# Squared-ReLU attention and an ELU MLP on one core: transposed score tiles turned a step earlier, loaded into up to four tiles, and no longer used in the last block

## The chip, the cores and the metric

The kernel runs on 1 core of one Trainium2 chip. The metric is device time in microseconds. The kernel before takes 2069.99 us, the median of 3 runs (2069.19 to 2071.52).

## The reference

```python
# u, v: (4, 3008, 256); z: (4, 3008, 64); moe_w_in: (256, 2048); moe_w_out: (2048, 256)
scores = (1.0 / S) * np.matmul(z, z.transpose(0, 2, 1))
attn = np.maximum(scores, 0.0) ** 2
x = (u * np.matmul(attn, v)).reshape(B * S, D)
h = x @ w_in
g = np.where(h > 0.0, h, np.exp(np.minimum(h, 0.0)) - 1.0)
out = g @ w_out
```

All arrays are float32. The score matrix of a batch is symmetric, since both of its factors are z.

## The kernel before

Every float32 operand of a matmul is split into a high part and the rest (`hi`, `lo`), and a product is the sum of three: high by high, high by low, low by high. The program has two stages. The attention stage takes the first 1096 us of the profiled execution, the MLP stage the rest; the change lies in the first.

The attention stage walks over 4 batches. A batch has 6 blocks of 496 or 512 columns of the score matrix (`BLOCKS`), and a block has 12 steps. A step handles one pair of 128-row strips, 256 rows, against the block's columns. So there are 288 steps, numbered by `s`; block 0 to block 5 of a batch follow each other, and `ORDER` says which pair stands at which place of a block. A step has three parts:

- `a_front(s)`: six matmuls of 64 rows, two beside each other, make the scores of the pair in PSUM tile `banks[s % 2]` (called `f`).
- `a_mid(s)`: ScalarE takes the ReLU out of `f` into half a row of SBUF (`r_two[s % 2]`), squares it there, ScalarE (pairs in `BY_ACT`) or VectorE makes `hi` from it, and VectorE subtracts to get `lo`. `hi` and `lo` each lie in a ring of three buffers.
- `a_back(s)`: 24 matmuls, twelve of them after each other with two running beside each other, add the pair's products with v to the four accumulators `acc`. `products` sets their order: the triple (c, d, q) names strip, half of the output and product (q = 1 is the one that reads `lo`). The last step of a block has nine in place of twelve.

Since the scores are symmetric, some of them exist already when a later block of the batch asks for them. Blocks 1 to 5 take the pairs in `LOADED` not from matmuls but from HBM, where `p_store` put them in an earlier block: 2, 4, 6, 6 and 4 pairs, 22 a batch, 88 in all. Such a loaded step has no `a_front`. `p_load(s)` fetches it with four DMAs of 128 KB, rows of 64 elements, into `r_two[s % 2]`; it is put two steps ahead of its use. In `a_mid(s)` VectorE then turns it by 32 x 32 squares (STREAM_TRANSPOSE, L478) into PSUM tile `banks[s % 2]`, ScalarE copies `hi` out of it, and VectorE subtracts.

Every engine runs its instructions in the order in which the program was written. The loop over `t` at L877 writes, for each step: `a_front(t)`, `a_back(t - 2)`, `a_mid(t)`, and then `background(t)`, the jobs that the table `at` gave to that step: loads and splits of v and z, the split of the MLP's weights (`w_split`, one or two VectorE instructions a step in blocks 1 to 3 of the first batches), and the splits and stores of what the attention stage yields (`x_parts`, `x_split`). All attention loads and most stores are issued by SyncE's queue, in order. At the second step of a block, `a_sums` adds the last block's accumulators (ScalarE copies two, VectorE adds two), before which the new block's first products can't start.

The last block of the last batch runs into the MLP stage: `START` lists the first MLP instructions and the products of steps 285 to 287 between them, and GpSimd's queue loads the MLP's inputs (`x_load`) into v's tiles as they come free.

## Time and profile before

| | |
|---|---|
| time, median of 3 runs | 2069.99 us |
| profiled execution: time, span | 2070.43 us, 2068.7 us |
| busy over the span: TensorE, VectorE, ScalarE | 94%, 83%, 72% |
| granted TensorE clock, mean | 0.981 |
| chain that ended last, by engine | TensorE 61%, ScalarE 14%, VectorE 10%, DMA 7%, issue 5% |
| DMA packets; of these under 512 B | 280431; 194528 |

The profile's page gives shares over the whole span, so it averages the two stages. Busy time of TensorE's matmuls contains time in which a matmul that has been started waits inside the pipeline, so it can't be read as work done. To see a stage, the busy time of each engine is asked for by windows; to see why an engine stands, the timeline of that window names, in brackets, the idle time ahead of an instruction and what ended it.

### The profile page before, as it was taken

To read this page: it belongs to the slowest core of one execution; us is meant where nothing else is said; L and a number is where in the kernel's file an instruction comes from. 1 tells how busy PE (TensorE), PEld (TensorE's weight loads), DVE (VectorE), ACT (ScalarE), POOL (GpSimd) and SP (SyncE) were. 2 spreads that over 40 slices of the span, in tenths; PEclk is the share of its full clock that TensorE was granted. 3 is DMA by queue.
4 is the path that set the end of the run, shared out by engine and by line. 5 is a ranking of instruction groups with operands and counts; after the bars stand their busy time and mean duration, and the time that the engine had idled before them with its cause. 6 is when DMAs were issued, how large, how long until landed. Compare 5 with 4: busy or idle time off the path is not lost.

```text
span 2068.7 us, 30697 instructions
## 1 busy us (share of the span) xinstructions
PE 1935.0 (94%) x12302; PEld 1584.9 (77%) x12302; DVE 1712.1 (83%) x1692; ACT 1493.0 (72%) x1629; POOL 60.8 (3%) x88
## 2 busy tenths in 40 slices
PE   9988889888899888998869999999999999999999
PEld 6876677766687666876657888888888888888887
DVE  7776677766678666876658999999999999999998
ACT  8765577656686556876548778788778787777887
POOL 0000000000000000000000000000000100000100
PEclk9999999999999999999989999999999999999999
DMA  7464756646566555556581123222221211211210
GB/s 237 164 172 119 186 176 217 185 118 166 147 232 196 147 128 155 213 183 150 119 218 50 45 75 105 61 74 78 76 71 50 71 60 30 91 60 30 73 38 20
DMA packets 280431, 247.60 MB, mean 120 GB/s; under 512 B 194528, under 2 KB 243936, under 8 KB 280288
## 3 DMA queue, kind: packets, MB, share of 16 engines
q1 hardware_dynamic: 260880, 202.39, 32.9%
q0 software_dynamic: 19264, 43.13, 7.6%
q8 instruction: 96, 1.57, 0.3%
q14 instruction: 47, 0.39, 0.1%
q10 hardware_dynamic: 144, 0.13, 0.0%
HBM read 138.17 MB, written 107.41 MB: 119 GB/s over the span
## 4 chain that ended last, share of the span: by engine, by line
PE 61%; ACT 14%; DVE 10%; DMA 7%; issue 5%; SPq 2%; DVEq 0%; ACTq 0%
PE p L674 12%; PE acc L392 11%; PE acc L693 8%; PE acc L691 8%; PE acc L692 8%; PE r L674 6%; ACT row L184 5%; DMA row<-p 5%; DVE row L181 4%; ACT row L487 4%; ACT row L484 4%; DVE f L478 4%; PE q L674 3%; PE f L392 3%; SPq L430 2%
## 5 line engine op out<-in xcount | busy, mean ns | idle before, releaser
L392 PE MATMUL acc<-row,x 64*128 64x496 f32 (+1 forms) x6768 | 845.8, 396 | 53.8 <-DVE row L181 31.9
L392 PEld LDWEIGHTS acc<-row,x 64*128 64x128 f32 x6768 | 659.5, 190 | 213.3 <-DVE row L181 56.9
L181 DVE TENSOR_TENSOR row<-row,row 128x992 fp32r<-128x992 f32 (+7 forms) x366 | 498.5, 1367 | 142.1 <-ACT row L184 134.0
L184 ACT ACTIVATE row<-p 128x496 f32<-128x496 f32 (+1 forms) x384 | 225.3, 587 | 130.1 <-PE p L674 120.4
L184 ACT ACTIVATE row<-f 128x992 fp32r<-128x992 f32 (+1 forms) x88 | 88.1, 1001 | 308.6 <-DVE f L478 288.7
L691 PE MATMUL acc<-row,wo_hi 128*128 128x496 f32 (+1 forms) x768 | 295.4, 385 | 0.0
L692 PE MATMUL acc<-row,wo_hi 128*128 128x496 f32 (+1 forms) x768 | 295.4, 385 | 0.0
L693 PE MATMUL acc<-row,wo_lo 128*128 128x496 f32 (+1 forms) x768 | 295.4, 385 | 0.0
L766 DVE SCALAR_TENSOR_TENSOR row<-row,row 128x1984 f32<-128x1984 f32 (+5 forms) x104 | 217.0, 2086 | 24.2 <-ACT row L764 23.8
L484 ACT ACTIVATE row<-f 128x992 f32<-128x992 f32 (+1 forms) x199 | 199.7, 1003 | 40.6 <-PE f L392 23.0
L760 ACT ACTIVATE row<-row 128x1984 f32<-128x1984 f32 (+5 forms) x104 | 182.2, 1752 | 58.4 <-DVE row L758 56.3
L768 DVE SCALAR_TENSOR_TENSOR row<-row,row 128x1984 f32<-128x1984 f32 (+5 forms) x103 | 216.0, 2097 | 0.2
L487 ACT ACTIVATE row<-row 128x992 f32<-128x992 f32 (+1 forms) x199 | 208.1, 1046 | 5.6
L181 DVE TENSOR_TENSOR row<-f,row 128x992 fp32r<-128x992 f32 (+1 forms) x88 | 105.1, 1195 | 100.3 <-ACT row L184 100.3
L762 ACT ACTIVATE row<-row 128x1984 f32<-128x1984 f32 (+5 forms) x104 | 181.6, 1747 | 0.5 <-DVE row L768 0.2
L764 ACT ACTIVATE row<-row 128x1984 f32<-128x1984 f32 (+5 forms) x104 | 181.4, 1746 | 0.3
L674 PE MATMUL p<-x,wi_hi 128*128 128x496 f32 (+1 forms) x576 | 175.0, 385 | 0.0
L693 PEld LDWEIGHTS acc<-row,wo_lo 128*128 128x128 f32 x768 | 144.2, 188 | 26.5
L692 PEld LDWEIGHTS acc<-row,wo_hi 128*128 128x128 f32 x768 | 144.2, 188 | 26.4
L691 PEld LDWEIGHTS acc<-row,wo_hi 128*128 128x128 f32 x768 | 144.2, 188 | 26.4
L184 ACT ACTIVATE row<-row 128x992 fp32r<-128x992 f32 (+3 forms) x157 | 143.7, 925 | 8.8 <-DVE row L768 2.9
L478 DVE STREAM_TRANSPOSE f<-row 128x1024 f32<-128x1024 f32 x88 | 110.5, 1256 | 42.8 <-DMA row<-p 40.2
(89 smaller groups left out, 1981.9 us busy)
## 6 DMA issues: line engine op xcount, KB each, us to landing
row<-p SPq DMA_DIRECT2D x352, 128.0 KB, 3.0
p<-row SPq DMA_DIRECT2D x72, 512.0 KB, 2.9
x<-x POOLq DMA_DIRECT2D x56, 496.0 KB, 4.6
x<-row SPq DMA_DIRECT2D x69, 248.0 KB, 2.7
x<-x POOLq DMA_DIRECT2D x28, 512.0 KB, 5.0
p<-row SPq DMA_DIRECT2D x24, 496.0 KB, 3.1
row<-in_v SPq DMA_DIRECT2D x44, 256.0 KB, 3.5
x<-row SPq DMA_DIRECT2D x38, 256.0 KB, 2.6
```

The lines of the kernel that those rows point to most:

```text
L181: nc.vector.tensor_tensor(out=lo, in0=src, in1=hi.bitcast(F32), op=ALU.subtract)
L184: nc.scalar.activation(out=out, in_=in_, func=AF.Copy)
L392: nc.tensor.matmul(out, w[rows], x[rows], start=start, stop=end)
L478: nc.vector.transpose(out=x.rearrange("p c (g j) -> p c g j", g=16), in_=t)
L484: nc.scalar.activation(out=x, in_=f[:, :, :n], func=AF.Relu, scale=1.0 / S)
L487: nc.scalar.activation(out=x, in_=x, func=AF.Square)
L674: nc.tensor.matmul(o, w, x, start=first and i == 0, stop=i == 2, skip_group_check=not first)
L691: nc.tensor.matmul(o, wh, hi, start=first, stop=False)
L692: nc.tensor.matmul(o, wh, lo, start=False, stop=False)
L693: nc.tensor.matmul(o, wl, hi, start=False, stop=last)
L766: stt(out=t, in0=m, scalar=1.0, in1=t, op0=ALU.add, op1=ALU.mult)
L768: stt(out=h, in0=h, scalar=0.0, in1=t, op0=ALU.max, op1=ALU.add)
```

## The change

`LOADED` loses its entries for block 5, whose `ORDER` becomes the natural one: all twelve of its steps make their scores by matmul. Block 1 of the last batch does so too. Loaded steps go from 88 to 70.

A planner, run while the program is written, now gives each step its tile (`t_of`) out of up to four: the two halves of `row3` as before, and in blocks 1 to 4 also the row `lr` and half of `row8` (the last batch has no `row8`). It also says when a load is issued (`at_of`): as early as four steps ahead, where a tile is free. In the plan that results every load is issued three or four steps ahead. `early(s)` holds for all 70.

The turning moves into `p_turn`. For an early step `s + 1` it is written into `a_mid(s)`, ahead of step s's subtraction, so it stands one step earlier in VectorE's order. The last two loaded steps of a block (30 in all) are turned into an SBUF tile (`x_of`) in place of a PSUM bank.

`products` puts those that read `lo` last. In the start of the program, four products of step 0 go ahead of step 1's scores. Loads and splits of z and v for the next batch move a little, since block 5's order is another.

```diff
-CLOSING = (0, 1, 2, 3, 6, 7, 4, 8, 9, 5, 10, 11)
+CLOSING = NATURAL
-LOADED = ((), (10, 11), (8, 9, 10, 11), (6, 7, 8, 9, 10, 11), (6, 7, 8, 9, 10, 11), (6, 7, 8, 9))
+LOADED = ((), (10, 11), (8, 9, 10, 11), (6, 7, 8, 9, 10, 11), (6, 7, 8, 9, 10, 11), ())
+AHEAD = 4
...
-    def products(late, edge):
-        if late:
-            return [(c, d, q) for q in (0, 2, 1) for c in range(2) for d in range(KD)]
-        if edge:
-            return [(c, d, q) for d in range(KD) for c in range(2) for q in range(3)]
-        return [(c, d, q) for c in range(2) for d in range(KD) for q in range(3)]
+    def products(i, first):
+        if i == NP - 1:
+            return [(c, d, q) for d in range(KD) for c, q in ((0, 0), (0, 2), (0, 1), (1, 0), (1, 1), (1, 2))]
+        if i == 0 and not first:
+            return [(c, d, q) for d in range(KD) for q in (0, 2, 1) for c in range(2)]
+        return [(c, d, q) for q in (0, 2, 1) for c in range(2) for d in range(KD)]
...
     def is_loaded(s):
-        return pair_of(s) in LOADED[s // NP % NI]
+        k = s // NP
+        return pair_of(s) in LOADED[k % NI] and k != (B - 1) * NI + 1
...
+    def p_turn(s):
+        order = "p (g c j) -> p c g j" if pair_of(s) == NP - 1 else "p (g j c) -> p c g j"
+        t = t_of[s].rearrange(order, g=16, c=2)
+        nc.vector.transpose(out=turned(s).rearrange("p c (g j) -> p c g j", g=16), in_=t)
+
+    def turned(s):
+        return pairs(x_of[s]) if s in x_of else banks[s % 2]
+
+    t_of, at_of, x_of = {}, {}, {}
+    tiles = r_two + [lr_row, cut(st_row, 0, 2)]
...
+    def early(s):
+        return s < NSTEP and is_loaded(s) and at_of[s] <= s - 3
...
-            x = banks[s % 2]
-            order = "p (g c j) -> p c g j" if pair_of(s) == NP - 1 else "p (g j c) -> p c g j"
-            t = r_two[s % 2].rearrange(order, g=16, c=2)
-            nc.vector.transpose(out=x.rearrange("p c (g j) -> p c g j", g=16), in_=t)
-            x = x[:, :, :n]
+            if not early(s):
+                p_turn(s)
+            if early(s + 1):
+                p_turn(s + 1)
+            x = turned(s)[:, :, :n]
             copy(hi[:, :, :n], x)
...
+            if early(s + 1):
+                p_turn(s + 1)
             nc.scalar.activation(out=x, in_=x, func=AF.Square)
...
-            at(s - 2, p_load, s)
+            at(at_of[s], p_load, s)
```

VectorE in the last four steps of block 3 of the first batch, before. `f0` and `f1` are the two PSUM banks, `row3` holds the two halves that loads fill, `row0` to `row2` hold `hi` and `lo`; the rows with `wi_` and `wt` are the split of the MLP's weights.

```order
L478 STREAM_TRANSPOSE f0_100<-row3_73 128x1024
L181 TENSOR_TENSOR row0_70<-f0_100,row0_70 128x2x496
L320 SCALAR_TENSOR_TENSOR wi_hi_63<-wm0_82,wt_84 128x512
L478 STREAM_TRANSPOSE f1_101<-row3_73 128x1024
L181 TENSOR_TENSOR row1_71<-f1_101,row1_71 128x2x496
L322 TENSOR_SCALAR wt_84<-wi_hi_63 128x512
L324 SCALAR_TENSOR_TENSOR wi_lo_64<-wt_84 128x512
L478 STREAM_TRANSPOSE f0_100<-row3_73 128x1024
L181 TENSOR_TENSOR row2_72<-f0_100,row2_72 128x2x496
```

Each turn is followed by the subtraction that reads the same bank. The same place now:

```order
L437 STREAM_TRANSPOSE f1_101<-row8_79 128x1024
L182 TENSOR_TENSOR row0_70<-f0_100,row0_70 128x2x496
L321 SCALAR_TENSOR_TENSOR wi_hi_63<-wm0_82,wt_84 128x512
L437 STREAM_TRANSPOSE lr_80<-row3_73 128x1024
L182 TENSOR_TENSOR row1_71<-f1_101,row1_71 128x2x496
L323 TENSOR_SCALAR wt_84<-wi_hi_63 128x512
L325 SCALAR_TENSOR_TENSOR wi_lo_64<-wt_84 128x512
L437 STREAM_TRANSPOSE row8_79<-row3_73 128x1024
L182 TENSOR_TENSOR row2_72<-lr_80,row2_72 128x2x496
```

The turn ahead of a subtraction is now that of the next step, and the last two write SBUF (`lr`, `row8`).

VectorE in the last block of the last batch, before, from the first step whose place is taken by a loaded pair:

```order
L478 STREAM_TRANSPOSE f0_100<-row3_73 128x1024
L181 TENSOR_TENSOR row2_72<-f0_100,row2_72 128x2x496
L181 TENSOR_TENSOR row4_74<-row4_74,high_81 128x496
L478 STREAM_TRANSPOSE f1_101<-row3_73 128x1024
L181 TENSOR_TENSOR row0_70<-f1_101,row0_70 128x2x496
L181 TENSOR_TENSOR row4_74<-row4_74,lr_80 128x496
L492 CAST row1_71<-row3_73 128x2x496
```

And now:

```order
L535 CAST row2_72<-row3_73 128x2x496
L182 TENSOR_TENSOR row2_72<-row3_73,row2_72 128x2x496
L182 TENSOR_TENSOR row4_74<-row4_74,row8_79 128x496
L182 TENSOR_TENSOR row0_70<-row3_73,row0_70 128x2x496
L182 TENSOR_TENSOR row4_74<-row4_74,high_81 128x496
L535 CAST row1_71<-row3_73 128x2x496
```

No turn is left there; `hi` of some steps is a cast by VectorE, of others a copy by ScalarE.

SyncE's queue around the same four steps of block 3, before (`p` are the stored scores, x4 is one loaded step):

```order
L577 DMA x0_1177<-high_81 128x512
L578 DMA x0_1177<-row4_74 128x512
L252 DMA row7_78<-in_zz 128x496
L287 DMA wm1_83<-in_w_in 128x1024
L430 DMA row3_73<-p01_107 32x16x64 x7
L430 DMA row3_73<-p00_106 32x16x64 x9
```

And now:

```order
L432 DMA row3_73<-p01_107 32x16x64 x4
L620 DMA x0_1174<-high_81 128x512
L621 DMA x0_1174<-row4_74 128x512
L432 DMA row8_79<-p01_107 32x16x64 x3
L432 DMA row8_79<-p00_106 32x16x64
L253 DMA row7_78<-in_zz 128x496
L288 DMA wm1_83<-in_w_in 128x1024
L432 DMA row3_73<-p00_106 32x16x64 x8
```

Two of the four loads have moved past the load of weights and the store of a split part, and one of them goes to `row8`.

## Rows read from the trace of the kernel before

**Rows 1.** Windows: blocks 0 to 5 of batch 1; blocks 1 on; the last block.

```profile
core 0: us, PE busy (x) PEld busy (x) DVE busy (x) ACT busy (x) POOL busy (x), PEclk, DMA share, GB/s
280.10:321.20 41.10, 40.72 (x356) 32.80 (x356) 34.16 (x50) 35.99 (x48) 0.00 (x0) 1.00 0.61 222
321.20:365.90 44.70, 41.93 (x354) 33.94 (x352) 34.17 (x46) 30.75 (x35) 0.00 (x0) 0.96 0.63 205
365.90:410.60 44.70, 39.88 (x344) 31.64 (x340) 34.25 (x43) 28.03 (x33) 0.00 (x0) 1.00 0.66 192
410.60:458.00 47.40, 39.36 (x312) 30.03 (x314) 32.49 (x40) 26.10 (x31) 0.00 (x0) 0.96 0.54 139
458.00:503.70 45.70, 40.26 (x324) 31.47 (x323) 30.68 (x34) 27.60 (x34) 0.00 (x0) 0.96 0.54 137
503.70:554.40 50.70, 41.08 (x314) 31.87 (x312) 32.98 (x42) 32.99 (x46) 0.00 (x0) 0.90 0.58 152
48.40:280.10 231.70, 200.06 (x1643) 160.99 (x1641) 162.35 (x198) 143.98 (x168) 0.00 (x0) 0.97 0.56 157
595.90:825.30 229.40, 201.31 (x1654) 157.90 (x1652) 163.79 (x201) 145.24 (x171) 0.00 (x0) 0.97 0.58 163
865.40:1042.60 177.20, 159.96 (x1332) 126.38 (x1328) 121.38 (x136) 114.96 (x132) 0.00 (x0) 0.97 0.55 156
1042.60:1096.30 53.70, 37.76 (x278) 28.93 (x276) 29.20 (x33) 27.76 (x34) 4.27 (x7) 0.84 0.67 174
```

**Rows 2.** Timeline of TensorE: steps made by matmul, 512 columns (start, us, engine, line).

```profile
18.78 3.10 PE L392 MATMUL acc<-row,x 64*128 64x512 f32 x24
21.50 1.06 PE L392 MATMUL f<-q,row 64*128 64x512 f32 x6
...
307.14 2.88 PE L392 MATMUL acc<-row,x 64*128 64x512 f32 x24
309.86 0.84 PE L392 MATMUL f<-q,row 64*128 64x512 f32 x6
310.54 1.75 PE L392 MATMUL acc<-row,x 64*128 64x512 f32 x14
```

**Rows 3.** Timeline of all engines: loaded steps of block 3, first batch.

```profile
171.65 3.35 PE L392 MATMUL acc<-row,x 64*128 64x496 f32 x24 [0.73 <-DVE row L181]
172.11 1.25 DVE L478 STREAM_TRANSPOSE f<-row 128x1024 f32<-128x1024 f32 x1
173.46 1.00 ACT L184 ACTIVATE row<-f 128x992 fp32r<-128x992 f32 x1 [3.09 <-DVE f L478]
174.49 1.19 DVE L181 TENSOR_TENSOR row<-f,row 128x992 fp32r<-128x992 f32 x1 [1.13 <-ACT row L184]
...
175.60 0.42 DVE L322 TENSOR_SCALAR wt<-wi_hi 128x512 int32<-128x512 int32 x1
...
175.74 2.73 PE L392 MATMUL acc<-row,x 64*128 64x496 f32 x22 [0.73 <-DVE row L181]
...
176.05 0.69 DVE L324 SCALAR_TENSOR_TENSOR wi_lo<-wt 128x512 fp32r<-128x512 int32 x1
176.66 1.25 DVE L478 STREAM_TRANSPOSE f<-row 128x1024 f32<-128x1024 f32 x1
```

**Rows 4.** Groups of instructions, attention stage: ScalarE's square and ReLU (busy, mean ns | idle).

```profile
L487 ACT ACTIVATE row<-row 128x992 f32<-128x992 f32 x112 | 115.7, 1033 | 3.1
L484 ACT ACTIVATE row<-f 128x992 f32<-128x992 f32 x112 | 110.8, 989 | 8.3 <-PE f L392 5.7 <-DMA p<-row 1.5 <-DVE row L551 0.5
```

**Rows 5.** Waits over the span (us in total, times, longest).

```profile
ACT row L184 <- DVE f L478: 288.7, 83, 8.5
DVE f L478 <- DMA row<-p: 40.2, 29, 5.9
```

**Rows 6.** DMA issues: size each, median us from issue to landing.

```profile
row<-p SPq DMA_DIRECT2D x352, 128.0 KB, 3.0
```

**Rows 7.** Timeline of the last block: a load issued, and a turn.

```profile
1053.41 2.23 SPq L430 DMA_DIRECT2D row<-p  x4
...
1061.14 1.26 DVE L478 STREAM_TRANSPOSE f<-row 128x1024 f32<-128x1024 f32 x1 [5.88 <-DMA row<-p]
```

More of the change, by code (lines that the diff above doesn't have):

```diff
@@ L150, in relu2_attention_elu_mlp @@
     w_ab, rraw_ring, sum_ring = Ring([cut(row, 0, 2)]), Ring([cut(row, 2)]), Ring([cut(row, 3)])
-    row = slot("row8", 4)
+    st_row = row = slot("row8", 4)
     st_ring = Ring([cut(row, a) for a in range(3)])
     temps = [cut(row, a) for a in range(4)]
-    row = slot("lr", 2)
+    lr_row = row = slot("lr", 2)
     lr_ring = Ring([cut(row, a) for a in range(2)])
@@ L427, in p_load @@
             c -= starts[j]
-            t = r_two[s % 2][a * Q:(a + 1) * Q].rearrange("p (g j) -> p g j", j=2 * Q)
+            t = t_of[s][a * Q:(a + 1) * Q].rearrange("p (g j) -> p g j", j=2 * Q)
             src = p_d[b, j][i0:i0 + 4 * P, c:c + 2 * Q]
             nc.sync.dma_start(out=t, in_=src.rearrange("(g r) j -> r g j", r=Q))
+    def p_turn(s):
[6 more added lines that the diff above has]
+    tiles = r_two + [lr_row, cut(st_row, 0, 2)]
+    used, held = [-9] * 4, {}
+    for now in range(NSTEP):
+        k = now // NP
+        n = 2 if k % NI in (0, 5) or k == (B - 1) * NI + 1 else 4 if k < (B - 1) * NI else 3
+        s = now + 1
+        if s < NSTEP and s % NP >= NP - 2 and is_loaded(s) and at_of.get(s, now) <= s - 3:
+            ok = [i for i in range(n) if held.get(i, -1) < now]
+            if len(ok) > (not is_loaded(now)):
+                i = min(ok, key=lambda i: used[i])
+                x_of[s] = tiles[i]
+                held[i] = used[i] = s
+        if not is_loaded(now):
+            i = min((i for i in range(n) if held.get(i, -1) < now), key=lambda i: used[i])
+            t_of[now], used[i] = tiles[i], now + (pair_of(now) in sent[k % NI])
+        for s in range(now + 1, min(now + AHEAD + 1, NSTEP)):
+            if is_loaded(s) and s not in t_of:
+                busy = sum(held.get(i, -1) > now for i in range(n))
+                direct = [not is_loaded(q) for q in range(now + 1, s + 1)]
+                room = n - (2 if any(a and c for a, c in zip(direct, direct[1:])) else 1 if any(direct) else 0)
+                if busy >= room or (n > 2 and s // NP % NI == 5):
+                    break
+                i = min((i for i in range(n) if held.get(i, -1) <= now), key=lambda i: used[i])
+                t_of[s], at_of[s] = tiles[i], now
+                held[i] = used[i] = s - (now <= s - 3)
+    assert all(s in t_of for s in range(NSTEP))
+    def early(s):
+        return s < NSTEP and is_loaded(s) and at_of[s] <= s - 3
     def a_front(s):
@@ L452, in a_mid @@
         n = cols(k)[1]
-        r = pairs(r_two[s % 2])
+        r = pairs(t_of[s])
         hi = pairs(hi_ring.next())
@@ L508, in w @@
             return vt[:, q // 2, c, d * P:(d + 1) * P]
-        for c, d, q in products(s < 4, i in (0, NP - 1))[part]:
+        for c, d, q in products(i, s == 0)[part]:
             if not last:
@@ L573, in x_split @@
         t = p_t[j][i]
-        hi = (w_hi if j < LATE else w_hi_late).next()[:, :n]
+        hi = (w_hi_late if j == LATE else w_hi).next()[:, :n]
         copy(hi, t)
@@ L791, in relu2_attention_elu_mlp @@
             at(2 * g - 4, l_load, 0, g)
-        at(2 * g - 1, l_hi, 0, g)
-        at(2 * g - 1, l_lo, 0, g)
+        at(2 * g - 2, l_hi, 0, g)
+        at(2 * g - 2, l_lo, 0, g)
     for b in range(1, B):
@@ L796, in relu2_attention_elu_mlp @@
         for p, t in enumerate((-8, -7, -6, -4, -2, 0, 1, 2, 3, 4, 5, 6)):
-            at(s0 + t - 3 - 2 * (p < 3), v_load, b, p)
+            at(s0 + max(t - 3 - 2 * (p < 3), -NP), v_load, b, p)
             at(s0 + t, v_split, b, p)
-        for g, t in ((3, -9), (0, -7), (1, -5), (4, -3), (2, -1), (5, 2)):
+        for g, t in ((0, -9), (1, -7), (2, -5), (3, -3), (4, -1), (5, 2)):
             at(s0 + t - 3, l_load, b, g)
@@ L879, in relu2_attention_elu_mlp @@
             k, p = divmod(t, NP)
-            if not (k and p == 3) and t != 2 and t < NSTEP - 2:
+            behind = t == 2 or t > 2 and is_loaded(t - 2) and t - 2 not in x_of
+            if t == 1:
+                a_back(0, slice(0, 4))
+            if behind and t < NSTEP - 1:
+                a_back(t - 2, slice(4 * (t == 2), None))
+            if not (k and p == 3) and t < NSTEP - 2:
                 a_front(t)
@@ L883, in relu2_attention_elu_mlp @@
                 a_front(t + 1)
-            if 2 <= t < NSTEP - 1:
+            if 2 < t < NSTEP - 1 and not behind:
                 a_back(t - 2)
-            if t == 2:
-                a_front(t)
             a_mid(t)
```

## The prediction

> **What bounds the kernel now.** I read the windows by block first, then the timeline inside one block, then the list of waits. In the windows the reader is to compare a block that has no loaded step with the ones that have. Batch 1's block 0 takes 41.1 us, blocks 1 to 4, with 2, 4, 6 and 6 loaded steps, 44.7, 44.7, 47.4 and 45.7, block 5 with 4 takes 50.7 and the last block of all 53.7 [rows 1]. Yet a loaded step has fewer matmuls, so these blocks ought to be shorter. VectorE is busy 30.7 to 34.3 us of each, ScalarE 26.1 to 36.0, the DMA engines at most 0.67: nobody is full [rows 1].
>
> The work of TensorE is read from starts, not from busy time. In the 512-column block the products of a step start at 307.14, the next scores at 309.86 and the next products at 310.54: 2.72 us for the 24 products, 0.68 for the scores, 3.40 a step [rows 2]. Scaled by 496/512 that is 2.64, 0.66 and 3.30. A block of 12 matmul steps at 512 columns, whose last step has 9 of 12 products, needs 12 x 3.40 - 0.68 = 40.1 us; block 0's 41.1 leaves 1.0 us for the change of block. So a block without loads is at TensorE's pace.
>
> In the run of loaded steps the timeline shows a chain instead. A turn starts at 172.11 and takes 1.25, ScalarE's copy of `hi` waits for it and takes 1.00, VectorE's subtraction waits 1.13 us for that copy and takes 1.19, and TensorE waits 0.73 for the subtraction before it can go on at 175.74 [rows 3]. The previous such start is at 171.65: 4.09 us a step where TensorE needs 2.64. Over the span ScalarE waits 288.7 us for turns, 83 times, while turns wait only 40.2 us for loads, 29 times out of 88 [rows 5]. The latency of the chain sets the pace, and the load is second.
>
> The Trainium skill ("Perfetto Trace Analysis", section Identifying the Most-Contended Engine) says that matmul busy time is no good measure of how near TensorE is to its limit. The trace bears it out: block 3 has 159 pairs of matmuls against block 0's 177 and shows nearly the same busy time, 39.36 us against 40.72 [rows 1]. Reading busy time as the floor of blocks 1 to 5 would leave 30.6 us a batch to win; counting products, as below, leaves 44.2.
>
> **The change, part by part.** *Floors.* With TensorE's pace and 1.0 us a block: block 1 (10 matmul steps, 2 loaded, 512 columns) 10 x 3.40 + 2 x 2.72 - 0.68 + 1.0 = 39.8; block 2 (8 and 4, 496 columns from here) 8 x 3.30 + 4 x 2.64 - 0.66 + 1.0 = 37.3; blocks 3 and 4 (6 and 6) 36.0 each; block 5, now 12 matmul steps, 39.9. Sum 189.0, against 233.2 for batch 1's blocks 1 to 5 [rows 1]. The added scores, 18 x 0.66 = 12 us in all, are inside these floors.
>
> *The turn a step ahead.* The turn of s + 1 now fills the 1.13 us in which VectorE waits for the copy of `hi`, and the next copy finds its tile turned. What is late next is VectorE's sum of work in a run of loaded steps: turn 1.25, subtraction 1.19, and one or two pieces of background, 0.42 and 0.69 [rows 3], so 2.86 to 3.55 a step, 3.2 in the mean, against TensorE's 2.64. Four such steps in a row cost 4 x 0.56 = 2.2 us, of which the two steps that TensorE may lag take some. I add 2.0 us to each of blocks 2, 3 and 4 and 0.7 to block 1, which has two.
>
> *The turn into SBUF* (30 of 70). No turn into SBUF stands in the trace. From below 0.69 (a VectorE pass over half the columns, as if it ran at twice the rate), from above 2.38 (twice the 1.19 of a subtraction) [rows 3]. I take the 1.25 of the turn into PSUM, the nearest. The ends are 30 x -0.56 = -17 and 30 x +1.13 = +34 us of VectorE; the low end saves nothing beyond the allowance, the high one falls in runs where VectorE is the later engine, so it stays in the range. ScalarE's copy out of SBUF I price at the square's 1.03 against 1.00 out of PSUM [rows 3, 4]: 30 x 0.03 = 0.9 us, hidden, since ScalarE is busy 26 to 31 us of those blocks.
>
> *High products first.* Same 24 matmuls. Step 1's products in the first block already have this order and take 18.78 to 21.50, 2.72 us, like the others [rows 2], so it costs nothing there. It gives TensorE 8 of 12 products, 1.8 us, before it needs `lo`, which is more than its 0.73 us wait. I count no gain of its own, since the floor assumes that this wait is gone.
>
> *Loads three or four steps ahead.* Four issues take 2.23 us [rows 7] and the last lands 3.0 us after its issue [rows 6]: 5.2 us. From the load's place, behind step s - 4, to the turn in step s - 1 VectorE has two whole steps, 5.3 us at 2.64, which is thin; SyncE reaches that place earlier where no store holds it, by up to a step, 7.9 us. Of the 70 loads four are put three steps ahead. Before, the load couldn't start until the turn two steps back had emptied its half row. I take 0, with the first rival for the other end. Behind a load that waits for its tile stand stores of split parts and loads of v, z, u and weights on SyncE's queue; their users come several steps later. 18 loads, so 72 issues, and a dozen stores go.
>
> *Block 5 without loads.* Four steps each lose a turn on VectorE (1.25) and get ReLU and square for a copy on ScalarE, 0.99 + 1.03 - 1.00 = 1.02 each [rows 3, 4]. ScalarE goes from 33.0 to 37.1 us of a 39.9 us block, so it nearly fills it: I add 1.0. Its low clock, 0.90 and in the last block 0.84 [rows 1], goes with the waits; block 0 shows 1.00.
>
> *The last block* before its first MLP matmul takes 53.7 us [rows 1]; one load issued at 1053.41 is waited for until 1061.14 [rows 7]. After: 11 scores and 11 sets of products of 496 columns, 36.3 - 0.66 + 1.0 + 1.5 (block 5's allowance and a half for the changeover) = 38.1. *Block 1 of the last batch* becomes like block 0, 41.1. *Start of the program, order of the z groups, loads of v:* the same work moved within slack, 0 for me, between -1 and +1 each.
>
> *The sum.* Blocks 1 to 5 after: 189.0 + 7.7 = 196.7. Batch 0: 231.7 - 196.7 = 35.0. Batch 1: 233.2 - 196.7 = 36.5. Batch 2: 229.4 - 196.7 = 32.7. Batch 3, blocks 1 to 4: 177.2 - (41.1 + 39.3 + 38.0 + 38.0) = 20.8. Last block: 53.7 - 38.1 = 15.6. Together 140.6 us. The profiled execution took 2070.4 us, its span and 1.7 around it, and lies 0.4 above the median; 2070.4 - 140.6 = 1929.8. I predict 1930 us.
>
> **The rivals.** *Loads become the wait.* A loaded step asks for 512 KB in 2.64 us, about 200 GB/s, near the 222 that the fullest window shows [rows 1]; also for it, the thin lead; against it, runs are four steps long and their loads are spread over more, and the DMA share in blocks 3 and 4 is 0.54. If the waits per load stay as they are, 40.2 / 88 = 0.46 us, 70 of them cost 32 us: 1962. The Trainium skill ("DMA: Bandwidth & Descriptors", section Specifications) asks for at least 512 B a transfer for full rate, and these runs are 64 elements, 256 B; that speaks for this rival, and no row here separates it.
>
> *VectorE becomes the bound.* If every loaded step costs its larger sum, 3.55 us, and nothing is caught up, 70 x 0.91 = 64 us, 26 of them in my allowances already: +38, 1968. For it: 34.3 busy us against block 2's floor of 37.3. Against: block 0 runs at TensorE's pace with the same 34.2 [rows 1].
>
> *The early turn doesn't do what it says*: ScalarE's copy is held by its buffer instead, which the products of three steps before must free, and runs keep 4.09 us a step. Then only the steps without loads gain: three blocks 5 of 9.8 each, 15.6 and 3.6 make 48: 2022. Against: three buffers at 2.64 us a set of products leave 7.9 us for a copy and a subtraction that take 2.2.
>
> *Slower.* The turn of s + 1 now stands ahead of the subtraction of s. A load that comes late holds back both, and TensorE, and all background work behind them. It decides from 140.6 / 70 = 2.0 us of such wait per load; at the 5.88 us once seen [rows 7], less the 1.8 that the high products cover, it would be 70 x 4.1 = 287 us: 2217. Against: the mean wait per load is 0.46 now.
>
> **How the numbers follow.** My forecast 0.65, with its own range 1900 (all allowances, 31 us, unneeded) to 1952; late loads 0.15; VectorE 0.10; no effect of the early turn 0.05; slower 0.03; and 0.02 for no change, by causes not named. The range 1900 to 1975 takes in the first three. What a measurement of this kernel can tell from no change is about 0.2%. Faster 0.95, same 0.02, slower 0.03.
>
> **What would show it.** Right: windows of blocks 3 and 4 at 37 to 39 us and block 5 near 41 with a clock of 0.98 or more; ScalarE's wait for turns under 40 us in total; starts of products in a run of loaded steps 2.7 to 3.3 us apart; the MLP's first matmul near 956 us, the MLP stage itself unchanged. Wrong: turns that wait for loads more than 40 us in total (first rival), a run at over 3.4 us a step with VectorE without gaps (second), `hi` copies that wait for TensorE (third), subtractions queued behind a waiting turn (fourth).

## The result and the profile after

| | before | after |
|---|---|---|
| time, median of 4 runs | 2069.59 us (2066.88 to 2071.52) | 1898.15 us (1894.24 to 1898.82) |
| ratio to before | 1 | 0.9169, 95% interval 0.9152 to 0.9185 |
| span of the profiled execution | 2068.7 us | 1896.1 us |
| first matmul of the MLP stage | 1096.3 us | 924.0 us |
| from there to the end | 972.4 us | 972.1 us |
| granted TensorE clock, mean | 0.981 | 1.000 |

The time fell by 171 us and all of it lies in the attention stage: the MLP stage starts 172.3 us earlier and takes what it took. The forecast was 1930 us with a range from 1900 to 1975; the measured time is just below the range's low end. The direction and the place were right, the size was not.

The windows of the changed kernel, blocks 0 to 5 of batch 1, then blocks 1 to 5 of batches 0, 1 and 2, blocks 1 to 4 of batch 3 and the last block, the same stretches as in [rows 1]:

```profile
core 0: us, PE busy (x) PEld busy (x) DVE busy (x) ACT busy (x) POOL busy (x), PEclk, DMA share, GB/s
233.10:276.80 43.70, 43.70 (x386) 35.87 (x385) 33.98 (x49) 35.83 (x47) 0.00 (x0) 1.00 0.55 195
276.80:314.90 38.10, 36.05 (x318) 29.11 (x316) 33.19 (x45) 30.63 (x34) 0.00 (x0) 1.00 0.70 227
314.90:353.40 38.50, 38.50 (x350) 32.44 (x348) 33.60 (x44) 27.92 (x33) 0.00 (x0) 1.00 0.72 194
353.40:388.70 35.30, 34.36 (x302) 27.89 (x302) 32.16 (x42) 26.27 (x31) 0.00 (x0) 1.00 0.81 204
388.70:424.20 35.50, 35.50 (x320) 29.79 (x318) 31.18 (x36) 27.93 (x33) 0.00 (x0) 1.00 0.63 157
424.20:463.80 39.60, 39.60 (x358) 33.18 (x356) 29.40 (x41) 36.83 (x49) 0.00 (x0) 1.00 0.48 153
...
45.50:233.10 187.60, 185.40 (x1646) 153.80 (x1645) 157.44 (x199) 147.98 (x172) 0.00 (x0) 1.00 0.64 179
276.80:463.80 187.00, 184.01 (x1638) 152.42 (x1636) 159.52 (x203) 149.58 (x176) 0.00 (x0) 1.00 0.66 187
505.50:693.30 187.80, 185.22 (x1652) 154.08 (x1650) 159.28 (x202) 149.60 (x176) 0.00 (x0) 1.00 0.64 183
735.50:889.00 153.50, 149.79 (x1324) 123.21 (x1322) 118.19 (x136) 117.44 (x135) 0.00 (x0) 1.00 0.59 161
889.00:924.00 35.00, 34.90 (x312) 28.82 (x308) 26.91 (x34) 31.28 (x38) 3.86 (x7) 1.00 0.72 233
```

The order of the blocks is now what their work says: those with six loaded steps are the shortest, 35.3 and 35.5 us, those without the longest. Before, the block without loaded steps was the shortest. TensorE is busy for 35.50 of 35.50 us in block 4, and since that alone proves nothing, the starts were counted too: where two matmuls in succession start more than 0.235 us apart, the excess over their usual 0.22 adds up to about 206 us in the attention stage before, what the lower granted clock cost included, and about 24 us after, none of it in the windows of blocks 4 and 5 above. (Block 0 is 1.6 us a batch longer than before, 127.6 against 122.7 us for three. A block is counted from the ReLU of its first step, which can come while TensorE is still at work on the block before, so a microsecond or two can pass from one block to its neighbour.)

The pace of a step made by matmul has stayed, as TensorE's timeline in a block of 512 columns shows (start, us, engine, line): 61.06 to 64.46 are the 3.40 us of [rows 2], of which the scores take 0.68.

```profile
61.06 2.88 PE L393 MATMUL acc<-row,x 64*128 64x512 f32 x24
63.78 0.84 PE L393 MATMUL f<-row,row 64*128 64x512 f32 x6
64.46 2.88 PE L393 MATMUL acc<-row,x 64*128 64x512 f32 x24
```

The timeline of all engines in block 3 of batch 0, the place of [rows 3] (start, us, engine, line, operation; in brackets the idle time ahead of it and what ended it):

```profile
143.78 13.56 PE L393 MATMUL acc<-row,x 64*128 64x496 f32 x120
...
149.78 1.25 DVE L437 STREAM_TRANSPOSE f<-row 128x1024 f32<-128x1024 f32 x1
150.94 1.17 DVE L182 TENSOR_TENSOR row<-f,row 128x992 fp32r<-128x992 f32 x1
151.13 1.00 ACT L185 ACTIVATE row<-f 128x992 fp32r<-128x992 f32 x1 [2.60 <-PE acc L393]
...
152.04 0.67 DVE L321 SCALAR_TENSOR_TENSOR wi_hi<-wm,wt 128x512 fp32r<-128x512 f32 x1
152.63 1.25 DVE L437 STREAM_TRANSPOSE lr<-row 128x1024 f32<-128x1024 f32 x1
...
153.80 1.15 DVE L182 TENSOR_TENSOR row<-f,row 128x992 fp32r<-128x992 f32 x1
153.99 1.03 ACT L185 ACTIVATE row<-lr 128x992 fp32r<-128x992 f32 x1 [1.86 <-DVE lr L437]
154.87 0.41 DVE L323 TENSOR_SCALAR wt<-wi_hi 128x512 int32<-128x512 int32 x1
155.32 0.69 DVE L325 SCALAR_TENSOR_TENSOR wi_lo<-wt 128x512 fp32r<-128x512 int32 x1
155.93 1.24 DVE L437 STREAM_TRANSPOSE row<-row 128x1024 f32<-128x1024 f32 x1
157.09 1.15 DVE L182 TENSOR_TENSOR row<-lr,row 128x992 fp32r<-128x992 f32 x1
```

VectorE has no bracket from 149.78 on: a subtraction follows the turn without a wait, where before it waited 1.13 us for the copy. Its turns start 2.85 and 3.30 us apart, the sums of what stands between them. ScalarE waits for TensorE or for VectorE, and that costs nothing: TensorE's first row is one stretch of 120 matmuls without a gap.

The waits over the span (us in total, times, longest), which answer to [rows 5]:

```profile
DVE row L182 <- ACT row L185: 96.6, 99, 3.4
...
ACT row L185 <- DVE f L437: 24.7, 16, 2.7
...
ACT row L185 <- DVE row L437: 11.7, 7, 2.3
...
DVE row L437 <- DMA row<-p: 5.9, 3, 3.2
...
ACT row L185 <- DVE lr L437: 3.7, 2, 1.9
```

ScalarE's wait for turns fell from 288.7 us to 40.1 (into `f`, `row` and `lr` together), just past the prediction's sign of being right, under 40. The turns' wait for loads fell from 40.2 us in 29 waits to 5.9 in 3 (and one of 0.2 for a load into `lr`); two of them, 5.6 us, lie in the last batch, which has a tile less. The loads themselves, 280 issues where there were 352, are no quicker (size each, median us from issue to landing), against the 3.0 of [rows 6]:

```profile
row<-p SPq DMA_DIRECT2D x216, 128.0 KB, 3.3
...
lr<-p SPq DMA_DIRECT2D x64, 128.0 KB, 3.9
```

In the last block nothing answers to [rows 7]: there is no load and no turn.

### The profile page after: what moved, and what is told of

Same layout as the page of the kernel before. It is cut to its first block, busy times and chain, and to the rows that moved or that the text cites. A ratio compares the mean times of both kernels' runs of the same rounds, so it can differ in the third digit from the quotient of the medians.

```text
span 1896.1 us, 30994 instructions
## 1 busy us (share of the span) xinstructions
PE 1878.6 (99%) x12410; PEld 1568.4 (83%) x12410; DVE 1691.9 (89%) x1692; ACT 1511.9 (80%) x1647; POOL 60.9 (3%) x88
## 2 busy tenths in 40 slices
DMA packets 240178, 231.96 MB, mean 122 GB/s; under 512 B 156321, under 2 KB 204705, under 8 KB 240033
## 4 chain that ended last, share of the span: by engine, by line
PE 87%; ACT 5%; DVE 3%; DMA 2%; issue 2%; SPq 1%; DVEq 0%; ACTq 0%
PE acc L393 31%; PE p L717 14%; PE acc L736 9%; PE acc L734 9%; PE acc L735 9%; PE r L717 7%; PE f L393 6%; PE q L717 3%; ACT row L185 1%; DVE row L182 1%; ACT row L530 1%; ACT row L525 1%; DMA row<-p 1%; DMA lr<-p 1%; SPq L432 1%
## 5 line engine op out<-in xcount | busy, mean ns | idle before, releaser
L393 PE MATMUL acc<-row,x 64*128 64x496 f32 (+1 forms) x6768 | 794.9, 384 | 10.1 <-DVE row L584 5.1
L393 PEld LDWEIGHTS acc<-row,x 64*128 64x128 f32 x6768 | 633.6, 184 | 142.6 <-DVE row L584 9.3
L182 DVE TENSOR_TENSOR row<-row,row 128x992 fp32r<-128x992 f32 (+6 forms) x381 | 511.0, 1347 | 94.7 <-ACT row L185 80.5
L803 ACT ACTIVATE row<-row 128x1984 f32<-128x1984 f32 (+5 forms) x104 | 182.2, 1753 | 58.6 <-DVE row L801 56.0
L525 ACT ACTIVATE row<-f 128x992 f32<-128x992 f32 (+1 forms) x182 | 182.7, 1004 | 56.1 <-PE f L393 26.7
L530 ACT ACTIVATE row<-row 128x992 f32<-128x992 f32 (+1 forms) x182 | 190.4, 1046 | 5.2
L717 PEld LDWEIGHTS p<-x,wi_hi 128*128 128x128 f32 x576 | 108.0, 188 | 20.5 <-ACT row L525 0.4
L813 DVE CAST row<-row 128x1984 fp32r<-128x1984 f32 (+3 forms) x98 | 113.9, 1162 | 3.3
L680 POOL DMA_DIRECT2D x<-x x84 | 60.7, 727 | 1731.8 <-PE acc L393 902.0
```

What stands on the lines that cost most here:

```text
L182: nc.vector.tensor_tensor(out=lo, in0=src, in1=hi.bitcast(F32), op=ALU.subtract)
L393: nc.tensor.matmul(out, w[rows], x[rows], start=start, stop=end)
L525: nc.scalar.activation(out=x, in_=f[:, :, :n], func=AF.Relu, scale=1.0 / S)
L530: nc.scalar.activation(out=x, in_=x, func=AF.Square)
L717: nc.tensor.matmul(o, w, x, start=first and i == 0, stop=i == 2, skip_group_check=not first)
L803: act(out=m, in_=h, func=AF.Relu, scale=-1.0)
```

## The experiments

Differences are between medians, against the changed kernel's 1898.15 us where nothing else is said; the ratio is to the kernel before on the same chip.

**The turn back in its own step, all else as changed.**

```diff
-                held[i] = used[i] = s - (now <= s - 3)
+                held[i] = used[i] = s
...
-            if not early(s):
-                p_turn(s)
-            if early(s + 1):
-                p_turn(s + 1)
+            p_turn(s)
...
-            if early(s + 1):
-                p_turn(s + 1)
             nc.scalar.activation(out=x, in_=x, func=AF.Square)
```

> The changed kernel, but each stored tile is turned in its own step again (ahead of that step's copy and subtraction); loads stay three or four steps ahead, the products high first, the last block without loads. Theory A (the turn a step ahead is what took the chain of turn, copy, subtraction off TensorE's path): VectorE's order is again turn 1.25, wait for the copy 1.13, subtraction 1.19 and background of 0.4 or more, so 4.0 us a loaded step against TensorE's 2.64; 70 steps lose up to 1.3 us each, less what TensorE's lag takes: 60 to 95 us slower than the changed kernel, 1955 to 1990 us. Rival B (the order of the products, by covering the wait for the low part, did most): under 25 us slower. Rival C (the early loads did most): under 25 us slower too.

Measured: 2007.53 us, ratio 0.9700 (0.9675 to 0.9724), 109 us slower, or 1.56 us for each of 70 loaded steps. (Since a tile is now held one step longer, the planner turns 27 steps into SBUF in place of 30; all loads are still three or four steps ahead, and no turn waits for one.) Of what the change gains this part alone carries more than half, and more than the 60 to 95 that I expected. The timeline of this kernel in the same run of loaded steps:

```profile
165.73 1.25 DVE L437 STREAM_TRANSPOSE f<-row 128x1024 f32<-128x1024 f32 x1
167.07 1.00 ACT L185 ACTIVATE row<-f 128x992 fp32r<-128x992 f32 x1 [3.50 <-DVE f L437]
...
168.10 1.19 DVE L182 TENSOR_TENSOR row<-f,row 128x992 fp32r<-128x992 f32 x1 [1.12 <-ACT row L185]
...
168.12 2.96 PE L393 MATMUL acc<-row,x 64*128 64x496 f32 x24 [2.06 <-ACT row L185]
...
169.81 1.25 DVE L437 STREAM_TRANSPOSE f<-row 128x1024 f32<-128x1024 f32 x1
```

Turns are 4.08 us apart, as before the change, though loads are early and high products first: VectorE's 1.12 us wait for the copy is back in a loop that VectorE closes itself, and TensorE waits 2.06 us.

**The old order of products.**

```diff
-        if i == NP - 1:
-            return [(c, d, q) for d in range(KD) for c, q in ((0, 0), (0, 2), (0, 1), (1, 0), (1, 1), (1, 2))]
-        if i == 0 and not first:
-            return [(c, d, q) for d in range(KD) for q in (0, 2, 1) for c in range(2)]
-        return [(c, d, q) for q in (0, 2, 1) for c in range(2) for d in range(KD)]
+        if first:
+            return [(c, d, q) for q in (0, 2, 1) for c in range(2) for d in range(KD)]
+        if i in (0, NP - 1):
+            return [(c, d, q) for d in range(KD) for c in range(2) for q in range(3)]
+        return [(c, d, q) for c in range(2) for d in range(KD) for q in range(3)]
...
-        for c, d, q in products(i, s == 0)[part]:
+        for c, d, q in products(i, s < 4)[part]:
```

> The changed kernel with the products in the old order, so that the second product of a step already reads the low part. Theory A: the low part is mostly ready when its step's turn on TensorE comes, 5 to 30 us slower than the changed kernel, spread over blocks with and without loads (each change of block would cost about 1 us, as block 0 of the kernel before shows: 41.1 us against 40.1). Rival B: the order is what keeps TensorE going in the loaded steps: over 50 us slower, all of it in blocks 1 to 4.

Measured: 1905.46 us, ratio 0.9207 (0.9183 to 0.9231), 7 us slower; the MLP stage starts 6.4 us later. A small part, as theory A has it; the intervals just touch, so its size is barely clear of noise.

**The new order alone, in the kernel before.**

```diff
-    def products(late, edge):
-        if late:
-            return [(c, d, q) for q in (0, 2, 1) for c in range(2) for d in range(KD)]
-        if edge:
-            return [(c, d, q) for d in range(KD) for c in range(2) for q in range(3)]
-        return [(c, d, q) for c in range(2) for d in range(KD) for q in range(3)]
+    def products(i, first):
+        if i == NP - 1:
+            return [(c, d, q) for d in range(KD) for c, q in ((0, 0), (0, 2), (0, 1), (1, 0), (1, 1), (1, 2))]
+        if i == 0 and not first:
+            return [(c, d, q) for d in range(KD) for q in (0, 2, 1) for c in range(2)]
+        return [(c, d, q) for q in (0, 2, 1) for c in range(2) for d in range(KD)]
...
-        for c, d, q in products(s < 4, i in (0, NP - 1))[part]:
+        for c, d, q in products(i, s == 0)[part]:
```

> The kernel before with one part of the change alone: the products of a step take the high part of a block first and the low part last; turns and loads stay in the step that uses them. Theory A: the loop of turn, copy and subtraction with VectorE as its pace sets the loaded steps, and it is as long in either order; TensorE starts earlier and then waits within the step: less than 15 us faster than before, 2055 to 2069. Rival: TensorE waits for the low part, and the order hides the subtraction (0.73 us) in each of 88 loaded steps: 64 us faster, near 2005.

Measured: 2073.27 us, ratio 1.0025 (1.0016 to 1.0035): no gain, a little slower. TensorE's products in this kernel, at the place of [rows 3]:

```profile
170.99 2.95 PE L392 MATMUL acc<-row,x 64*128 64x496 f32 x24 [2.06 <-ACT row L184]
...
175.07 2.93 PE L392 MATMUL acc<-row,x 64*128 64x496 f32 x24 [1.13 <-ACT row L184]
```

The wait within the step has become one for the copy ahead of it, and the starts are 4.08 us apart instead of 4.09. That TensorE waited 0.73 us for `lo` was true and worth nothing: the wait only moved.

**Loads at most two steps ahead.**

```diff
-AHEAD = 4
+AHEAD = 2
...
-        return s < NSTEP and is_loaded(s) and at_of[s] <= s - 3
+        return s < NSTEP and is_loaded(s) and at_of[s] <= s - 2
```

(The planner's two other thresholds of three steps become two as well.)

> The changed kernel with loads put two steps ahead in place of three or four; the turn stays one step ahead. Theory A: a load needs 2.2 us of issue and 3.3 to 3.9 us to land, and the turn now stands one step behind the load's place, so VectorE stands at the turn, with the subtraction of the step before behind it: 1 to 2.5 us for each of the 70 loaded steps, 70 to 175 us slower than the changed kernel. Against (loads had their time anyway, since SyncE runs ahead of VectorE): under 20 us slower.

Measured: 1926.62 us, ratio 0.9312 (0.9292 to 0.9332), 28.5 us slower, 0.41 us a load: below theory A's 70 and above the other side's 20, so neither had it. Turns wait 58.6 us for loads in 30 waits, where the changed kernel has 6.1 in 4; about half of that reaches the end. The early turn still pays with loads two steps ahead: this kernel is 81 us faster than the one with early loads and the turn in its own step.

**The last two turns of a block into PSUM too.**

```diff
-                x_of[s] = tiles[i]
-                held[i] = used[i] = s
+                pass
```

> The changed kernel with the last two loaded steps of each block turned into a PSUM bank, as the others, in place of SBUF. Theory A: at the 15 ends of a block with loads the next block's scores wait for the bank until the subtraction two steps before is done; 0.5 to 2 us each, 8 to 30 us slower than the changed kernel, all of it where blocks 1 to 4 end. Against: no difference over 4 us, since the products of the loaded steps are put ahead of the scores there.

Measured: 1919.06 us, ratio 0.9271 (0.9250 to 0.9293), 21 us slower, as theory A has it. Block 1 takes 40.8 us in place of 38.5 in the mean of three batches, block 3 39.4 in place of 35.7, block 4 37.1 in place of 35.4. A turn a step ahead needs a bank that the next block's scores also need; SBUF takes it out of that queue. It shows in ScalarE's wait for scores in `f`: 74.8 us in all, where the changed kernel has 38.8. (The loop puts the products of a step that lies in a bank ahead of the scores of two steps on, and those of a step in SBUF behind them. That order is part of the change too; here it changes for these 30 steps together with the bank, and no run tells the two apart.)

**No loads in block 5, in the kernel before.**

```diff
-CLOSING = (0, 1, 2, 3, 6, 7, 4, 8, 9, 5, 10, 11)
+CLOSING = NATURAL
...
-LOADED = ((), (10, 11), (8, 9, 10, 11), (6, 7, 8, 9, 10, 11), (6, 7, 8, 9, 10, 11), (6, 7, 8, 9))
+LOADED = ((), (10, 11), (8, 9, 10, 11), (6, 7, 8, 9, 10, 11), (6, 7, 8, 9, 10, 11), ())
```

(Loads of v and z follow the block's new order.)

> The kernel before with one part of the change alone: block 5 makes all its scores by matmul (with the order of v and z splits that this needs). Theory A: the three inner blocks 5 fall from 50 us to 41 and the last one from 53.7 to about 38, as their four waiting turns go: 38 to 48 us faster than the kernel before, 2021 to 2031 us; the rest of the gain is in blocks 1 to 4. Rival (the blocks without loads gain from the new order of products more than from the missing loads): under 30 us faster.

Measured: 2021.00 us, ratio 0.9773 (0.9759 to 0.9786), 47 us faster than before. Block 5 falls from 50.2 to 38.4 us, the last from 53.7 to 34.9. The like of it in the prediction is the sum of its third rival, 48, less the 3.6 for block 1 of the last batch, which here keeps its loads: some 45.

**Block 5's loads put back, turned in their own step.**

```diff
-LOADED = ((), (10, 11), (8, 9, 10, 11), (6, 7, 8, 9, 10, 11), (6, 7, 8, 9, 10, 11), ())
+LOADED = ((), (10, 11), (8, 9, 10, 11), (6, 7, 8, 9, 10, 11), (6, 7, 8, 9, 10, 11), (6, 7, 8, 9))
```

(With block 5's old order and the loads of z that go with it.)

> The changed kernel with block 5's four loaded pairs put back in their old order; with two tiles there the loads are two steps ahead and the turns in their own step, so this undoes the last block's part alone. Theory A: each of the 16 steps loses the 1.6 us that the turn in its own step costs (109 us for 70) and saves 0.66 of scores, and some wait for loads comes back: 15 to 45 us slower than the changed kernel. Rival (the last block's loads cost nothing once products come high first): 10 us faster.

Measured: 1943.43 us, ratio 0.9404 (0.9387 to 0.9420), 45 us slower, at the upper edge of theory A. Block 5 takes 52.0 us, the last 48.9. So this part and the early turn hardly overlap: taken from either end it is worth 45 to 47 us.

**The same, turned a step ahead though only two tiles are free there.**

```diff
-        return s < NSTEP and is_loaded(s) and at_of[s] <= s - 3
+        return s < NSTEP and is_loaded(s) and at_of[s] <= s - (2 if s // NP % NI == 5 else 3)
```

> As the run with block 5's loaded pairs put back, but their turns a step ahead too, with loads two steps ahead. Theory A: TensorE sets the pace, so each of the 16 loaded steps saves 0.66 us of scores, 10.6 in all; loads two steps ahead cost 28.5 / 70 = 0.41 us each, 6.5; so 4 us faster than the changed kernel, between 10 faster and 15 slower. Rival (in block 5 the queue of loads for the next batch holds them up, as in the kernel before): over 15 us slower.

Measured: 1982.09 us, ratio 0.9587 (0.9574 to 0.9600): 84 us slower than the changed kernel, where I expected 4 faster, and 39 us slower than the run above. A miss, and the most useful run. Block 5 takes 60.6 us in the mean of three batches. That of the first batch (`lr<-in_zz` loads z for the next batch):

```profile
213.73 1.26 DVE L437 STREAM_TRANSPOSE f<-row 128x1024 f32<-128x1024 f32 x1 [4.56 <-DMA row<-p]
...
216.57 0.84 DVE L182 TENSOR_TENSOR row<-lr,row 64x256 fp32r<-64x256 f32 x2
...
217.48 0.35 SPq L223 DMA_DIRECT2D lr<-in_zz  x1
...
219.36 2.58 SPq L432 DMA_DIRECT2D row<-p  x4
...
226.60 1.26 DVE L437 STREAM_TRANSPOSE f<-row 128x1024 f32<-128x1024 f32 x1 [6.78 <-DMA row<-p]
227.77 0.66 DVE L535 CAST row<-row 128x992 fp32r<-128x992 f32 x1
...
228.49 6.96 PE L393 MATMUL acc<-row,x 64*128 64x496 f32 x40 [6.28 <-DVE row L535]
```

The load is issued at 219.36 and the turn stands at the head of VectorE's queue for 6.78 us. Behind it stand the cast and the subtraction of the step before, whose input ScalarE had finished at 221.38; TensorE waits 6.28 us for that cast. Over the span turns into `f` wait 75.8 us for loads, 14 times.

Why the load is so late is in the lines above it, and in the waits of SyncE's queue in this block:

```profile
SPq L223 <- DVE row L182: 22.9, 4, 8.2
SPq L432 <- DVE row L182: 8.6, 2, 5.5
```

SyncE issues in order. The load of z at 217.48 waits until VectorE has read `lr` (the subtraction at 216.57), that subtraction stands behind the turn at 213.73, which itself waited for a load, and the next load of scores stands behind the load of z. So each late load makes the next one late: a loop of VectorE and SyncE, and the rival that I named before the run. The other inner blocks 5 show the same, 23.7 and 22.9 us of SyncE's waits at L223. In the last block, which loads no z, SyncE waits 19.4 us for VectorE at the loads of scores themselves (L432). It is also the prediction's slower rival, seen on the chip: 75.8 us are 4.7 for each of the 16 loads, past the 2.0 a load from which, by the prediction, the change would lose; with loads two steps ahead in blocks 1 to 4 it was 58.6 / 70 = 0.8. Two steps ahead is thus not in itself too late. What decides is whether the load's issue has to wait for VectorE.

**More work on VectorE: half a subtraction more in each loaded step (the same values again).**

```diff
+        if is_loaded(s):
+            sub(lo[:, 0, :n], x[:, 0], hi[:, 0, :n])
```

> The changed kernel with the first half of the subtraction done twice in each of the 70 loaded steps: one more VectorE pass of 496 columns, 0.67 us alone, 0.6 behind another. It asks whether VectorE is the later engine in the runs of loaded steps, as my allowance of 2 us a block said. Theory A (TensorE's lag of two steps and VectorE's free time in the other steps take it): under 15 us slower than the changed kernel, most of it in blocks 2 and 3, where VectorE has the weights to split too. Rival (VectorE sets the pace there): 70 x 0.6 = 42 us slower, 35 to 50.

Measured: 1918.58 us, ratio 0.9278 (0.9265 to 0.9291), 20.4 us slower: 0.29 us of each 0.6 added, between the two. In batches 0 to 2 it costs block 1 nothing (38.4 in place of 38.5), block 2 2.5 us of the 2.4 added, block 3 2.4 of 3.6, block 4 0.8 of 3.6.

**Less work on VectorE in block 2: four casts made by ScalarE.**

```diff
-BY_ACT = ((3, 7, 11), (1, 3, 5, 7, 9), (1, 3, 5, 7), NATURAL, NATURAL, (1, 3, 5, 10))
+BY_ACT = ((3, 7, 11), (1, 3, 5, 7, 9), NATURAL, NATURAL, NATURAL, (1, 3, 5, 10))
```

> The changed kernel with one line different: in block 2 the high part of the four even pairs is taken by ScalarE (a copy, some 1.03 us) and no longer by VectorE (a cast, 0.67 to 0.69 us), which frees VectorE of 2.7 us in that block and gives ScalarE 4.1. Theory A: VectorE is the engine that is tight in block 2 (the experiment with more work on VectorE cost 2.5 us there), and ScalarE has room: block 2 falls from 38.3 to 36 to 37.5, 2 to 10 us faster than the changed kernel, 1888 to 1896 us. Rival: block 2 is at its floor of TensorE already and the 2.5 us were only the other side of an edge: no difference, 1896 to 1900. Third: the copies stand in the way of the ReLU and square on ScalarE: slower, 1900 to 1910.

Measured: 1901.22 us, ratio 0.9190 (0.9173 to 0.9206). The intervals overlap, so the 3 us to the changed kernel are no difference that can be told; block 2 goes from 38.3 to 38.9 us. Theory A falls; between the other two the run doesn't decide. More work on VectorE costs time in block 2 and less gains none: VectorE is at the edge there, not past it, and TensorE sets the pace.

**One more loaded step in block 4, with and without those casts moved.**

```diff
-ORDER = (NATURAL, NATURAL, NATURAL, MIXED, MIXED, CLOSING)
+FOURTH = (0, 1, 2, 4, 3, 6, 5, 7, 8, 9, 10, 11)
+ORDER = (NATURAL, NATURAL, NATURAL, MIXED, FOURTH, CLOSING)
...
-LOADED = ((), (10, 11), (8, 9, 10, 11), (6, 7, 8, 9, 10, 11), (6, 7, 8, 9, 10, 11), ())
+LOADED = ((), (10, 11), (8, 9, 10, 11), (6, 7, 8, 9, 10, 11), (4, 6, 7, 8, 9, 10, 11), ())
```

The first run has this beside the line of the last experiment, the second has this alone.

> As the kernel with the casts moved, and one more pair (4) of block 4 is loaded instead of computed: seven loaded steps and five scores in place of six and six. Theory A: TensorE has no idle time left in block 4, so its time is its work: one score less in each of four batches, 4 x 0.66 = 2.6 us faster than the kernel with the casts moved. Rival: the run of five loaded steps at VectorE's 3.2 us each against TensorE's 2.6 to 2.7 uses up the two steps that TensorE lags: 1 to 2 us a block slower, 4 to 8 us in all.

> The changed kernel with one edit: pair 4 of block 4 is loaded as well, seven loaded steps and five scores there; the casts of block 2 stay on VectorE as in the changed kernel. Theory A: TensorE is without idle time in block 4, so that a score less is a score's time less in each of four batches, 4 x 0.66 = 2.6 us: 1894 to 1896.5 us, ratio to before 0.9145 to 0.916. The pair of runs with the casts moved differs by 4.8 us, which would make it 1893. Rival: no difference from the changed kernel (0.9169), because the longer run of loaded steps gives it back.

Measured: with the casts moved 1896.43 us, ratio 0.9169 (0.9155 to 0.9183), 4.8 us under its neighbour; alone 1895.35 us, ratio 0.9153 (0.9139 to 0.9168), 2.8 us under the changed kernel where 2.6 were expected. Block 4 takes 1.2 and 1.0 us less in batches 0 to 2, but block 3 1.5 us more in both, so where the gain comes from is not settled. The version alone has the lowest median of all, but its interval overlaps that of the changed kernel: it isn't shown to be faster.

## Why the prediction was off, step by step

**The bound before: right.** The chain from turn to copy to subtraction set the pace of the loaded steps, and the load was second. With the turn back in its own step the 4.08 us a step and 109 us return. The forecast's excess of 4.09 - 2.64 = 1.45 us a step would give 102 for 70 steps; 1.56 was measured.

**The floors: right.** From block 1 of a batch to block 1 of the next the changed kernel takes 231.3, 228.7 and 230.0 us, 230.0 in the mean (from the starts 45.5, 276.8, 505.5 and 735.5 of the windows). The prediction's products and scores alone are 40.1 for block 0 and 184.0 for blocks 1 to 5, 224.1 in all; the 5.9 above are as many as the 1.0 assumed for each of six changes of block. The total is right, its place isn't: by the starts of matmuls about 4 us of a batch are gaps, most of them where block 0 goes over into block 1 and block 2 into block 3, where TensorE waits for the sums of the last accumulators (1.62 us once, at 282.55) or for a ReLU (1.68 us, at 587.93). The other 2 us are not located.

**The failed step: the allowances for VectorE and ScalarE, 7.7 us a batch.** The prediction put a batch at 196.7 and block 0 at 40.9 in the mean of [rows 1] and the blocks' starts, 237.6; the chip took 230.0, 7.6 less. Over three batches that is 22.8 of the 31.7 us by which the sum of gains, 140.6, fell short of 172.3. VectorE's sum was right where it was read, in block 3: 2.85 and 3.30 us from turn to turn where 2.86 to 3.55 were given. Two things were wrong. The first is that block 4, which has no split of the weights, was charged the same. Its last four turns in the first batch:

```profile
181.23 1.25 DVE L437 STREAM_TRANSPOSE f<-row 128x1024 f32<-128x1024 f32 x1
...
184.35 1.25 DVE L437 STREAM_TRANSPOSE f<-lr 128x1024 f32<-128x1024 f32 x1
...
186.60 1.22 DVE L437 STREAM_TRANSPOSE row<-row 128x1024 f32<-128x1024 f32 x1
...
189.39 1.23 DVE L437 STREAM_TRANSPOSE lr<-row 128x1024 f32<-128x1024 f32 x1
```

They are 3.12, 2.25 and 2.79 us apart, 2.72 in the mean, hardly more than TensorE's 2.64. The second is that a deficit was charged nearly at once. TensorE works two steps behind, 5.3 us of products; four steps at 0.56 use up 2.2 of it, and steps made by matmul, where TensorE needs 3.30, give it back. The prediction named this lag and then took only 0.2 of the 2.2 off for it.

The traces show what is left of the lag. Take the time from the end of a loaded step's subtraction to the first product that reads its result (the matmuls counted in their order, 24 a step and 18 in a block's last step). In batches 0 to 2 it is never under 0.7 us in block 1, 1.3 in block 3 and 2.1 in block 4; in block 2 it falls to between 0.05 and 0.5. So in these blocks TensorE hardly waits for a loaded step, and only in block 2 is the lag used up. The probes agree: VectorE's added work costs block 2 all of it, block 3 two thirds, block 4 a fifth and block 1 nothing, and less work on VectorE gains nothing in block 2.

ScalarE's 1.0 in block 5 wasn't needed either: it is busy 36.83 us, close to the 37.1 forecast, in 39.6, and TensorE has no gap.

**The rest of the shortfall.** Blocks 1 to 4 of the last batch took 153.5 us against 156.4 forecast, 2.9 less where 6.0 had been allowed. There, with a tile less, two turns waited for a load (2.34 and 3.22 us), and behind each of them TensorE waited for a subtraction, 1.00 us at 809.97 and 1.49 at 885.69. The last block took 35.0 against 38.1: neither its 1.5 nor the 1.0 for a change of block came. The start of the program gained 2.9 us (48.4 to 45.5), priced at nothing within 1; a run of the kernel before without block 5's loads has 49.0 there, one with the new order of products 48.9, so it belongs to the new start. Two things are new there, four products of step 0 ahead and the splits of z a step earlier, and neither was tried alone; the runs that share this start have 45.2 to 47.8. The range's low end allowed for the allowances alone, 31 us, and had no room for these.

**The turn into SBUF: right in price, blind for its worth.** It takes 1.23 us in the mean of 30, where 1.25 was taken and 0.69 and 2.38 were the ends. But it was treated as a cost only; without it, and with the order of products that goes with it, the kernel is 21 us slower.

**High products first: right.** No gain of its own was counted; it is some 7 us in the changed kernel and none in the kernel before.

**The loads: right, with the reason sharper.** Taken at 0, with 32 us for the other end. Two steps ahead they cost 28.5 us; three or four steps ahead turns wait 6.1 us in all. In block 3 of batch 1 the share of the DMA engines rose from 0.54 to 0.81, and over the span the loads' landing went from 3.0 to 3.3 and 3.9 us. That block is among the shortest all the same. The Trainium skill ("DMA: Bandwidth & Descriptors", section Specifications) asks for at least 512 B a transfer for line rate; 156321 of the changed kernel's 240178 packets are smaller. No run here has larger ones to compare, so what that costs a load isn't shown.

**Block 5 and the last block: right in the main.** They bring 47 us alone in the kernel before, where the prediction's sum for its third rival has some 45 without block 1 of the last batch. The clock went with the waits as said: 1.00 in every window above, where block 5 had 0.90 and the last 0.84.

**The slower rival** didn't occur in the changed kernel, nor with loads two steps ahead in blocks 1 to 4 (28.5 us slower than the changed kernel, far faster than before). In block 5, with two tiles and loads whose issue waits for VectorE, it did.

The parts undone one at a time give 109, 45, 28, 21 and 7 us, 210 in all against 171 gained, so they overlap. That the early turn uses the early load and the free bank is a likely reason; no run undoes two of these at once to show it.

## What to carry to other kernels

Before charging an engine that is late by half a microsecond a step, compare the run's whole deficit with the work queued ahead of the engine that sets the pace, and charge only what is over; read the deficit in each block by itself, since a block with less work beside may have none; a probe that adds known work shows where that edge is. A short wait beside a loop on two engines says nothing of its worth: find the engine whose own next instruction closes the loop and fill its idle time. Whoever moves an instruction up in an in-order queue must look at what it waits for, since everything behind it waits too, and ask whether that in turn waits for this queue: here the same edit brought 109 us in blocks 1 to 4, and cost 39 us in block 5, where a load's issue waited for instructions that stood behind the turn.

## What the runs showed of the hardware that was not expected

A turn of 128 x 1024 takes 1.23 us into SBUF and 1.25 into PSUM (means of 30 and 40). Instructions on VectorE overlap a little: the turn at 149.78 lasts 1.25 us and the subtraction behind it starts at 150.94, 1.16 later. And with the DMA engines at 0.81 and 204 GB/s in block 3, loads of 128 KB still landed in 3.3 and 3.8 us in the median of that window.
